# A seven-tile ring of weights for the second layer, and two read-backs issued a step later

## The chip, the cores and the metric

The kernel runs on one core of one Trainium2 chip. The metric is the device time of one execution in microseconds (us), as the median of the runs of a kernel. One further execution was taken with the hardware profiler; all rows shown here come from it.

## The reference

Causal attention in blocks of 64 over 4 batches of 8 heads (576 positions, head size 64) gives 2304 tokens of 512 numbers. Two gated layers follow, with 1536 hidden numbers each:

```python
x = attention(q, k, v)                      # 2304 x 512
x = (x @ w_a * (x @ w_b)) @ w_out           # first layer
xn = x / sqrt(mean(x * x) + 1e-6) * rms_g   # second layer
g = xn @ w_gate
y = (g * sigmoid(g) * (xn @ w_val)) @ w_out
```

All of it is fp32. The kernel reaches that accuracy by splitting each operand of a product into a high and a low part and adding three products: high by high, high by low, low by high.

## The kernel before

**Stages.** Tokens lie on the free axis. The first layer runs in five blocks of 512, 256, 512, 512 and 512 tokens, with the attention of the next batch beside each block but the last. The second layer runs in three blocks of 768 tokens. The table `blocks` holds all eight, and `before_fc` is called ahead of every tile of weights.

**Second layer.** `moe2` forms the two products of a pair of hidden groups by a scheme with seven half-size products instead of eight (`product`, lines L499 to L501 and L527 to L529). A half (`wi`) of a pair takes two tiles of weights: the even tile carries slots 0 to 3, the odd one slots 4 to 6. A slot is six matmuls of 384 columns, so an even tile feeds 24 matmuls and an odd one 18. The results are added on VectorE (L521 to L547, with ScalarE's copy L518 ahead of them), gated (L552 to L559) and split (L98, L108). Every three hidden groups `output` (L431 to L433, 72 matmuls) adds into `acc`; the results of a block leave by L744, `finish`.

**Weights.** `fetch_ab` loads a tile of the second layer from DRAM (`ab<-wc`, L227): 1024 KB for an even tile, 768 KB for an odd one. The pool `wab` has three tiles. `before_fc(fc)` fetches tile `fc + 2`, whose place is that of tile `fc - 1`. `fetch_o` (L231) loads 1536 KB of output weights at tiles 0, 4, 12 and 20 of a block.

**Norm.** While a block runs, the generator `normed` prepares the next block of the second layer, one step at each tile (two steps at each tile of the first layer). It loads the tokens (`xf`, L679), squares and sums them, puts the row of means in DRAM (`row<-sq`, L699), reads it back across partitions (`sm<-row`, L701), takes the root, puts the roots in DRAM (`row<-sm`, L709) and reads them back to all partitions (`y<-row`, L710). Then four multiplications `xf` (L714) and four sums (L636) follow on VectorE, and the split of seven operands. Each read-back stands right behind its write on the queue of SyncE (SP), which issues every transfer of this kernel in order.

**Order.** The tile framework simulates the program and writes out one order for each engine; an instruction waits there for its inputs and holds up what stands behind it. `behind(ins, "gate")` keeps an instruction behind the last gating instruction on VectorE in that order, without a semaphore.

**Memory.** `wab` and `stage` (tiles for decoding the weights, unused in the second layer) are opened for the whole kernel. The pools of the first layer are closed when the second begins, and `hp2`, `tp2` and `acc2` open on their place.

Of the kernel before, what the change touches and what calls it, by code (L numbers as in the profile page):

```python
# [9 lines left out]
F32R = mybir.dt.float32r  # L10
# [6 lines left out]
P = 128  # L17
# [28 lines left out]
def tile_attention_moe_moe(  # L46
# [13 lines left out]
    pe, act, dve, pool, sp = nc.tensor, nc.scalar, nc.vector, nc.gpsimd, nc.sync  # L60
# [5 lines left out]
    KC = DM // P  # L66
# [9 lines left out]
    const = ctx.enter_context(tc.tile_pool(name="const", bufs=1))  # L76
    wab = ctx.enter_context(tc.tile_pool(name="wab", bufs=3))
    wop = ctx.enter_context(tc.tile_pool(name="wop", bufs=2))
    stage = ctx.enter_context(tc.tile_pool(name="stage", bufs=2))
    dram = ctx.enter_context(tc.tile_pool(name="dram", bufs=1, space=bass.MemoryType.DRAM))  # L80
    x2_dram = dram.tile([P, KC, NT], F32, name="x2_dram")

# [114 lines left out]
        elif y == (1 if kind == "ab" else TF - 1):  # L197
            sp.dma_start(out=wab_dram[f] if kind == "ab" else wo_dram[layer][f], in_=t.bitcast(F32))

    quarters = {}  # L200

    def combine(pair, y, src):

# [14 lines left out]

    def fetch_ab(layer, n):

        t = wtiles["ab", n] = wab.tile([P, 4, KC * P], F32R, tag="ab", name="ab")
        if layer == 0:
            sp.dma_start(out=t.bitcast(F32), in_=wab_dram[n])
        else:
            pair, y, a = n // 4, n // 2 % 2, n % 2 * 4
            z = min(a + 4, NC)
            sp.dma_start(out=t[:, 0:z - a, :].bitcast(F32), in_=wc_dram[pair][y][:, a:z, :])  # L227
# [360 lines left out]
    BMAX = [max(n for l, _, n, _ in blocks if l == x) for x in range(2)]  # L588

    make_identity(nc, ident)  # L590
    first_layer = ctx.enter_context(ExitStack())
    hp = first_layer.enter_context(tc.tile_pool(name="hp", bufs=TF + 1))
    tp = first_layer.enter_context(tc.tile_pool(name="tp", bufs=2))
    xs = first_layer.enter_context(tc.tile_pool(name="xs", bufs=1))
# [80 lines left out]
    def normed(t0, n, parts):  # L675

        xr, ps_r = rms["sb"], rms["ps"]
        x = xr.tile([P, KC, BMAX[1]], F32, tag="xf", name="xf")[:, :, 0:n]
        sp.dma_start(out=x, in_=x2_dram[:, :, t0:t0 + n])  # L679
        sq = xr.tile([P, BMAX[1]], F32, tag="sq", name="sq")[:, 0:n]  # L680
        y = xr.tile([P, BMAX[1]], F32, tag="y", name="y")[:, 0:n]
        behind(act.activation(sq, x[:, 0, :], AF.Square), "hh")
        for c in range(1, KC):
            act.activation(y, x[:, c, :], AF.Square)
            dve.tensor_tensor(sq, sq, y, ALU.add)
            if c == 2:
                yield None
        sh = xr.tile([P, BMAX[1]], F32R, tag="sh", name="sh")[:, 0:n]
        sl = xr.tile([P, BMAX[1]], F32R, tag="sl", name="sl")[:, 0:n]
        split(sh, sl, sq, act, dve, "hh")  # L690
        yield None

        row, small = dram.tile([2, n], F32, name="row"), xr.tile([P, 3, n // P], F32, tag="sm", name="sm")
        for o, w in parts:
            ps = ps_r.tile([P, 512], F32, tag="r", name="r")
            pe.matmul(ps[:, 0:w], rms["ones"], sh[:, o:o + w], start=True, stop=False)
            pe.matmul(ps[:, 0:w], rms["ones"], sl[:, o:o + w], start=False, stop=True)
            dve.tensor_scalar(sq[0:1, o:o + w], ps[0:1, 0:w], 1.0 / DM, 1e-6, ALU.mult, ALU.add)
        sp.dma_start(out=row[0:1, :], in_=sq[0:1, :])  # L699
        v, r, t = (small[:, x, :] for x in range(3))  # L700
        sp.dma_start(out=v, in_=row[0, :].rearrange("(p n) -> p n", p=P))  # L701
        yield None
        behind(act.activation(r, v, AF.Sqrt), "hh")
        dve.reciprocal(r, r)
        dve.tensor_tensor(t, r, r, ALU.mult)
        dve.tensor_tensor(t, t, v, ALU.mult)
        dve.tensor_scalar(t, t, -0.5, 1.5, ALU.mult, ALU.add)
        dve.tensor_tensor(r, r, t, ALU.mult)
        sp.dma_start(out=row[1, :].rearrange("(p n) -> p n", p=P), in_=r)  # L709
        sp.dma_start(out=y, in_=row[1, :].partition_broadcast(P))  # L710
        yield None
        for c in range(KC):
            behind(
                dve.scalar_tensor_tensor(x[:, c, :], x[:, c, :], rms_g[:, c:c + 1], y, ALU.mult, ALU.mult),  # L714
                "gate",
            )
            yield None
        for b in sums_of(x):
            yield b
        if t0 == blocks[NB_FIRST][1]:  # L720

            res = {}
            for _ in split_sums(b, res):
                yield res
# [4 lines left out]
    for at, (layer, t0, n_tok, parts) in enumerate(blocks):  # L729
        following = blocks[at + 1] if at + 1 < len(blocks) else None  # L730
        with_attention = at + 1 < NB
        if layer == 1 and blocks[at - 1][0] == 0:
            first_layer.close()
            hp = ctx.enter_context(tc.tile_pool(name="hp2", bufs=6))
            tp = ctx.enter_context(tc.tile_pool(name="tp2", bufs=1))
            accs = ctx.enter_context(tc.tile_pool(name="acc2", bufs=1))
        acc = accs.tile([P, KC, BMAX[layer]], F32, tag="acc", name="acc")
        norm = normed(*following[1:]) if following and following[0] == 1 else iter(())
        got = {}

        def finish(dm, o, n, acc=acc, layer=layer, t0=t0):
            cols = slice(t0 + o, t0 + o + n)
            dst = x2_dram[:, dm, cols] if layer == 0 else out[dm * P:(dm + 1) * P, cols]
            sp.dma_start(out=dst, in_=acc[:, dm, o:o + n])  # L744

        n_tiles = (FC, 2 * FC)[layer]

        def before_fc(fc, n_tiles=n_tiles, at=at, layer=layer, following=following, norm=norm, got=got):
            if at == 0:
                if fc > 0:  # L750
                    for _ in range(TF):
                        if prepared[0] < len(w_pieces) // 2:
                            prepare()
            else:
                if layer == 1 and fc in (0, 4, 12, 20):
                    fetch_o(layer, (0, 4, 12, 20).index(fc))
                if layer == 0 and fc % TF == 0:
                    fetch_o(layer, fc // TF)
                if fc + 2 < n_tiles:
                    fetch_ab(layer, fc + 2)  # L760
                if layer == 0:
                    n = sum(BACKGROUND[:at]) + min(BACKGROUND[at], BACKGROUND[at] * (fc + 1) // (FC - 3))
                    while prepared[0] < len(w_pieces) // 2 + n:
                        prepare()
            if following and fc + 2 >= n_tiles:
                fetch_ab(following[0], fc + 2 - n_tiles)
            if fc >= 1:
                for _ in range(FC * 2 // n_tiles):
                    got["x"] = next(norm, None) or got.get("x")

        def before_last(at=at, layer=layer, following=following, got=got, norm=norm):
            if following is None:
                return iter(())
            if following[0] == 0:
                last = (following[1] + following[2] - 1) // S
                while done.get(last, 0) < H:
                    att.step()
            if following[0] == 0:
                got["split"] = split_of(*following[1:3])
            elif layer == 0:  # L780
                got["split"] = got["x"]
                assert len(got["x"]) == 7 and next(norm, 0) == 0
            else:
                got["split"] = {}
                assert "T4" in got["x"]
                return split_sums(got["x"], got["split"])
            return iter(())

        main = Stream((moe1, moe2)[layer]((hp, tp), nxt, parts, mm, acc, finish, before_fc, before_last))
        a0 = att.spent  # L790
        while main.step():
            while (
                with_attention
                and done.get(at + 1, 0) < H
                and att.spent - a0 < PACE[at] * main.spent
            ):
                with tc.high_priority(AHEAD[at]):
                    att.step()
        nxt = got.get("split")
        if at == NB - 2:  # L800
            while att.step():
                pass
            attn.close()
            xr = ctx.enter_context(tc.tile_pool(name="xr", bufs=1, side="right"))
            rms["sb"] = xr
            rms["ps"] = ctx.enter_context(tc.tile_pool(name="psr", bufs=2, space=PSUM, side="right"))
            mm_pools.append(ctx.enter_context(tc.tile_pool(name="psm2", bufs=3, space=PSUM, side="right")))
            ones = xr.tile([P, P], F32, name="ones")
            rms["ones"] = xr.tile([P, P], F32R, name="ones_r")
            pool.memset(ones, 1.0)  # L810
            dve.tensor_copy(rms["ones"], ones)
# [58 lines left out]
```

## Time and profile before

| | |
|---|---|
| median of 3 runs | 1141.39 us (1140.19 to 1143.38) |
| profiled execution, its own time | 1145.9 us |
| its span, first to last instruction | 1144.0 us |
| mean granted TensorE clock | 0.987 |
| TensorE matmuls busy | 1085.2 us, 95% |
| VectorE busy | 747.2 us, 65% |
| ScalarE busy | 525.3 us, 46% |
| GpSimd busy | 466.5 us, 41% |

Matmuls overlap and their ends are modelled, so the busy time of TensorE overstates how full it is. The second layer runs from about 702 us to the end.

### The profile page before, as it was taken

Reading aid. Unit: us, or ns where it says so; the run is one execution under the profiler, and the core shown is the slowest. Engines: PE = TensorE matmul, PEld = TensorE weight load, DVE = VectorE, ACT = ScalarE, POOL = GpSimd, SP = SyncE. Lnnn points to the kernel's source line nnn. Section 1 sums busy time; section 2 is a strip of 40 time slices with the busy share of each in tenths; the row PEclk is TensorE's granted clock in tenths of the full one; section 3 lists DMA queues with packets and bytes.
Section 4 is the critical chain, followed back from the end, with each engine's and each line's share of the span. In section 5 each row is a group of like instructions: output and inputs, shape, how many; then the busy total and the mean of one; then the engine's idle time right before and its main releaser. Section 6 shows DMA issues by size and latency. Waiting matters only on the chain.

```text
span 1144.0 us, 16235 instructions
## 1 busy us (share of the span) xinstructions
PE 1085.2 (95%) x5780; PEld 958.1 (84%) x5780; DVE 747.2 (65%) x1379; ACT 525.3 (46%) x1142; POOL 466.5 (41%) x460
## 2 busy tenths in 40 slices
PE   6889989999999999899999999999998899999998
PEld 4567767789888778688888778999998899999998
DVE  5888897856776767544646585755775755765564
ACT  5877876746556665325325434431423222223120
POOL 5766677534555665345434351221312212222120
PEclk9999999899999999999999999999999999999999
DMA  6544887868886867969979877845666457475551
GB/s 173 185 152 162 253 267 248 297 235 275 300 291 228 281 244 267 345 243 364 345 266 346 332 283 270 274 177 190 251 242 213 166 184 243 166 262 193 184 213 56
DMA packets 74280, 276.48 MB, mean 242 GB/s; under 512 B 25684, under 2 KB 33364, under 8 KB 56279
## 3 DMA queue, kind: packets, MB, share of 16 engines
q1 hardware_dynamic: 74198, 275.44, 68.4%
q8 instruction: 46, 0.75, 0.3%
q14 instruction: 36, 0.29, 0.1%
HBM read 218.77 MB, written 56.64 MB: 241 GB/s over the span
## 4 chain that ended last, share of the span: by engine, by line
PE 59%; DMA 15%; DVE 11%; POOL 6%; ACT 5%; issue 3%; SPq 0%; POOLq 0%; ACTq 0%; DVEq 0%
PE mm L433 7%; PE mm L431 7%; PE mm L432 7%; DMA ab<-wc 5%; PE mm L469 5%; PE mm L471 5%; PE mm L470 5%; PE mm L499 5%; DMA st<-in_w_ab_dram 5%; PE mm L500 5%; PE mm L501 5%; PE s L305 3%; POOL x L139 2%; DMA st<-in_w_o_dram 2%; DVE st L138 2%
## 5 line engine op out<-in xcount | busy, mean ns | idle before, releaser
L431 PE MATMUL mm<-hh,o 128*128 128x384 f32 (+2 forms) x528 | 190.5, 363 | 6.2 <-ACT hh L98 3.3
L432 PE MATMUL mm<-hh,o 128*128 128x384 f32 (+2 forms) x528 | 187.9, 357 | 0.0
L469 PE MATMUL mm<-xh,ab 128*128 128x512 f32 (+1 forms) x480 | 181.9, 382 | 3.0 <-DVE xh L100 1.0
L470 PE MATMUL mm<-xl,ab 128*128 128x512 f32 (+1 forms) x480 | 182.1, 380 | 0.0
L471 PE MATMUL mm<-xh,ab 128*128 128x512 f32 (+1 forms) x480 | 180.6, 377 | 0.0
L433 PE MATMUL mm<-hl,o 128*128 128x384 f32 (+2 forms) x528 | 179.5, 356 | 0.6 <-DVE hl L108 0.6
L108 POOL TENSOR_TENSOR hl<-g,hh 128x384 fp32r<-128x384 f32 (+2 forms) x76 | 89.6, 1179 | 174.2 <-ACT hh L98 157.1
L98 ACT ACTIVATE hh<-g 128x384 fp32r<-128x384 f32 (+2 forms) x132 | 71.1, 553 | 157.1 <-DVE g L559 95.7
L554 POOL TENSOR_TENSOR asb<-c,sig 128x384 f32<-128x384 f32 x36 | 36.8, 1022 | 224.4 <-ACT sig L552 204.1
L329 POOL TENSOR_SCALAR pp<-pp,st 128x64 f32<-128x64 f32 (+3 forms) x144 | 87.3, 621 | 78.5 <-DVE st L326 44.5
L431 PEld LDWEIGHTS mm<-hh,o 128*128 128x128 f32 x528 | 100.4, 190 | 18.6 <-ACT hh L98 5.0
L499 PE MATMUL mm<-hT,ab 128*128 128x384 f32 x288 | 99.4, 345 | 11.1 <-DMA ab<-wc 10.1
L469 PEld LDWEIGHTS mm<-xh,ab 128*128 128x128 f32 x480 | 91.4, 191 | 20.2 <-DVE acc L440 1.7
L305 PE MATMUL s<-ks,qz 128*128 128x384 f32 (+4 forms) x284 | 97.4, 433 | 11.4 <-ACT pp L314 11.2
L433 PEld LDWEIGHTS mm<-hl,o 128*128 128x128 f32 x528 | 99.8, 190 | 9.7 <-DVE hl L108 1.3
L432 PEld LDWEIGHTS mm<-hh,o 128*128 128x128 f32 x528 | 100.6, 190 | 8.8 <-issue 1.6
L471 PEld LDWEIGHTS mm<-xh,ab 128*128 128x128 f32 x480 | 91.1, 190 | 16.4 <-issue 0.7
L470 PEld LDWEIGHTS mm<-xl,ab 128*128 128x128 f32 x480 | 91.2, 190 | 16.2 <-issue 0.7
L440 DVE SCALAR_TENSOR_TENSOR acc<-mm,acc 128x384 f32<-128x384 f32 (+2 forms) x132 | 74.6, 588 | 42.4 <-PE mm L433 42.2
L501 PE MATMUL mm<-hT,ab 128*128 128x384 f32 x288 | 97.1, 337 | 0.0
L500 PE MATMUL mm<-lT,ab 128*128 128x384 f32 x288 | 96.9, 337 | 0.0
L314 ACT ACTIVATE pp<-s,st 128x288 f32<-128x288 f32 (+8 forms) x142 | 71.3, 505 | 40.5 <-DVE st L308 36.7
(128 smaller groups left out, 2343.5 us busy)
## 6 DMA issues: line engine op xcount, KB each, us to landing
ab<-wab SPq DMA_DIRECT2D x48, 1024.0 KB, 7.2
o<-wo SPq DMA_DIRECT2D x28, 1536.0 KB, 7.7
ab<-wc SPq DMA_DIRECT2D x36, 1024.0 KB, 6.9
ab<-wc SPq DMA_DIRECT2D x36, 768.0 KB, 4.4
st<-in_w_ab_dram SPq DMA_DIRECT2D x48, 512.0 KB, 4.6
wc<-bg SPq DMA_DIRECT2D x12, 1792.0 KB, 8.0
wab<-ab SPq DMA_DIRECT2D x12, 1024.0 KB, 4.9
st<-in_w_o_dram SPq DMA_DIRECT2D x24, 512.0 KB, 4.5
```

The source lines that it names most:

```text
L108: eng_lo.tensor_tensor(lo, src, hi.bitcast(F32), ALU.subtract)
L305: pe.matmul(ps[:, 0:z - a], qz[m % 2][:, b], ks[m][:, a:z], start=True, stop=True)
L329: pool.tensor_scalar(t, t, s[:, 10 + y:11 + y], 1.0, ALU.mult, ALU.mult)
L431: pe.matmul(ps[:, 0:n], wh, hh, start=(y == 0), stop=False)
L432: pe.matmul(ps[:, 0:n], wl, hh, start=False, stop=False)
L433: pe.matmul(ps[:, 0:n], wh, hl, start=False, stop=(y == TF - 1))
L469: pe.matmul(ps[:, 0:n], wh[:, a:z], xhc, start=(c == 0), stop=False)
L470: pe.matmul(ps[:, 0:n], wh[:, a:z], xlc, start=False, stop=False)
L471: pe.matmul(ps[:, 0:n], wl[:, a:z], xhc, start=False, stop=(c == KC - 1))
L499: pe.matmul(ps[:, 0:n], wh, xh[:, c, :], start=(c == 0), stop=False)
L500: pe.matmul(ps[:, 0:n], wh, xl[:, c, :], start=False, stop=False)
L501: pe.matmul(ps[:, 0:n], wl, xh[:, c, :], start=False, stop=(c == 1))
```

## The change

`stage` moves into the group of pools that is closed when the second layer begins. A pool `wab2` of four tiles opens on its place, and the tiles of the second layer go round seven places: three of `wab`, four of `wab2`. In the second layer `before_fc(fc)` fetches tile `fc + 6` instead of `fc + 2`; at the first tile of its first block it also fetches tiles 2 to 5, so that five fetches stand there. In `normed` each of the two read-backs is issued one step after its write, and stands behind the gating instruction of that step in the planned order. The norm so has two steps more, and all that follows the read-backs comes one or two steps later.

```diff
-    stage = ctx.enter_context(tc.tile_pool(name="stage", bufs=2))
+    first_layer = ctx.enter_context(ExitStack())
+    stage = first_layer.enter_context(tc.tile_pool(name="stage", bufs=2))
...
-    quarters = {}
+    quarters, rings, n_ring = {}, [], [0]
...
-        t = wtiles["ab", n] = wab.tile([P, 4, KC * P], F32R, tag="ab", name="ab")
+        ring = wab
+        if layer == 1:
+
+            n_ring[0] += 1
+            if n_ring[0] % 7 > 3 or n_ring[0] % 7 == 0:
+                ring = rings[0]
+        t = wtiles["ab", n] = ring.tile([P, 4, KC * P], F32R, tag="ab", name="ab")
...
-    first_layer = ctx.enter_context(ExitStack())
...
-        sp.dma_start(out=v, in_=row[0, :].rearrange("(p n) -> p n", p=P))
+        yield None
+        behind(sp.dma_start(out=v, in_=row[0, :].rearrange("(p n) -> p n", p=P)), "gate")
...
-        sp.dma_start(out=y, in_=row[1, :].partition_broadcast(P))
+        yield None
+        behind(sp.dma_start(out=y, in_=row[1, :].partition_broadcast(P)), "gate")
...
             first_layer.close()
+            rings.append(ctx.enter_context(tc.tile_pool(name="wab2", bufs=4)))
...
-                if fc + 2 < n_tiles:
-                    fetch_ab(layer, fc + 2)
+                if layer == 1 and rings and fc == 0 and blocks[at - 1][0] == 0:
+                    for i in range(2, 6):
+                        fetch_ab(layer, i)
+                ahead = 2 if layer == 0 else 6
+                if fc + ahead < n_tiles:
+                    fetch_ab(layer, fc + ahead)
...
-            if following and fc + 2 >= n_tiles:
-                fetch_ab(following[0], fc + 2 - n_tiles)
+            ahead = 2 if layer == 0 else 6
+            if following and fc + ahead >= n_tiles:
+                fetch_ab(following[0], fc + ahead - n_tiles)
```

## Rows read from the trace of the kernel before

**Rows 1.** Busy time by stage (three blocks of the second layer; one full stretch).

```profile
core 0: us, PE busy (x) PEld busy (x) DVE busy (x) ACT busy (x) POOL busy (x), PEclk, DMA share, GB/s
702.00:848.00 146.00, 143.48 (x814) 140.68 (x813) 98.32 (x171) 48.37 (x86) 30.43 (x26) 1.00 0.63 221
848.00:994.00 146.00, 135.91 (x756) 133.39 (x754) 93.40 (x164) 42.31 (x79) 30.55 (x26) 0.98 0.58 204
994.00:1143.00 149.00, 145.96 (x831) 143.41 (x830) 80.83 (x150) 33.63 (x68) 24.69 (x24) 1.00 0.50 182
760.00:780.00 20.00, 20.00 (x116) 19.81 (x116) 7.15 (x14) 5.01 (x10) 2.03 (x2) 1.00 0.49 171
```

**Rows 2.** Waits: who waited for whom, us in total, times, longest.

```profile
PE mm L499 <- DMA ab<-wc: 11.5, 9, 3.1
...
PEld mm L499 <- DMA ab<-wc: 13.1, 18, 3.5
```

**Rows 3.** Timeline of TensorE: start, duration, instruction, idle time before it and its releaser.

```profile
884.87 0.34 PE L501 MATMUL mm<-hT,ab 128*128 128x384 f32 x1
888.35 0.45 PE L499 MATMUL mm<-hT,ab 128*128 128x384 f32 x1 [3.15 <-DMA ab<-wc]
...
897.81 0.41 PE L499 MATMUL mm<-hT,ab 128*128 128x384 f32 x1 [2.43 <-DMA ab<-wc]
```

**Rows 4.** Busy time by stage, two stretches behind such waits; columns as in the first group.

```profile
862.00:865.00 3.00, 3.00 (x12) 3.00 (x11) 1.66 (x3) 0.00 (x0) 0.00 (x0) 0.51 0.04 7
889.00:892.00 3.00, 3.00 (x12) 3.00 (x12) 3.00 (x7) 0.82 (x2) 0.00 (x0) 0.56 0.08 33
```

**Rows 5.** Timeline of SP's queue at the second block's begin.

```profile
851.14 0.33 SPq L744 DMA_DIRECT2D out_dram<-acc  x1
853.45 1.54 SPq L227 DMA_DIRECT2D ab<-wc  x2
...
876.24 0.32 SPq L709 DMA_DIRECT2D row<-sm  x1
881.26 0.32 SPq L710 DMA_DIRECT2D y<-row  x1
881.67 22.97 SPq L227 DMA_DIRECT2D ab<-wc  x6
```

**Rows 6.** Issues from 690 us on: count, size, median us to landing.

```profile
ab<-wc SPq DMA_DIRECT2D x35, 1024.0 KB, 6.9
ab<-wc SPq DMA_DIRECT2D x36, 768.0 KB, 4.4
...
y<-row SPq DMA_DIRECT2D x2, 384.0 KB, 8.3
```

**Rows 7.** Timeline of VectorE, second block.

```profile
886.46 2.87 DVE L714 SCALAR_TENSOR_TENSOR xf<-xf,rms_g,y 128x768 f32<-128x768 f32 x3 [4.07 <-DMA y<-row]
...
896.99 0.55 DVE L543 TENSOR_TENSOR c<-p,mm 128x384 f32<-128x384 f32 x1
```

**Rows 8.** Timeline of SP's queue where the layers meet.

```profile
689.54 0.57 SPq L679 DMA_DIRECT2D xf<-x_dram  x1
691.30 5.76 SPq L227 DMA_DIRECT2D ab<-wc  x2
...
706.66 2.09 SPq L744 DMA_DIRECT2D x_dram<-acc  x3
711.03 1.88 SPq L227 DMA_DIRECT2D ab<-wc  x2
```

**Rows 9.** Timeline of ScalarE there.

```profile
698.30 0.85 ACT L684 ACTIVATE y<-xf 128x768 f32<-128x768 f32 x1 [3.62 <-DMA xf<-x_dram]
...
706.01 0.49 ACT L518 ACTIVATE p<-mm 128x384 f32<-128x384 f32 x1
```

**Rows 10.** Busy time by stage in the first layer's last block; columns as in the first group.

```profile
620.00:640.00 20.00, 19.78 (x87) 15.88 (x86) 9.94 (x22) 10.44 (x19) 8.64 (x8) 1.00 0.98 376
660.00:680.00 20.00, 17.84 (x71) 13.52 (x70) 18.98 (x19) 9.45 (x14) 13.22 (x8) 0.94 0.65 246
```

## The prediction

> **What bounds the kernel now.** I read the busy time by stage first. Where nothing disturbs TensorE, 116 matmuls take 20.00 us, that is 0.1724 us from start to start [rows 1]. The three blocks of the second layer show 814, 756 and 831 matmuls in 146, 146 and 149 us. At 0.1724 us they would need 140.3, 130.3 and 143.3 us. So TensorE loses 5.7, 15.7 and 5.7 us, 27 us in all, and only this can be won there: TensorE bounds the layer, and VectorE is busy for 98 of 146 us at most. The count of instructions on TensorE doesn't change.
>
> The list of waits says what the loss is made of. The first matmul of a tile (L499) idled nine times for the tile's transfer, 11.5 us together, and the weight load did so 18 times [rows 2]. The timeline shows how to size one wait: the last start before it is 884.87, the next 888.35, so 3.48 us instead of 0.17, a loss of 3.31 where the list shows 3.15; the first matmul then takes 0.45 instead of 0.34 us [rows 3]. So each of the nine costs about 0.27 us more than its idle time: 11.5 + 9 x 0.27 = 13.9 us. For the nine times in which only the weight load idled I take 0.25 us each, the same overhead: 2.2 us. Transfers that come late thus cost 16.1 us.
>
> Behind the two longest the clock fell. From 862 to 865 us and from 889 to 892 us only 12 matmuls fit into 3 us, at a granted clock of 0.51 and 0.56, which is the 1.2 GHz level [rows 4]; at 0.1724 us they need 2.07 us. That is 0.93 us in each. The low spacing reaches beyond these 3 us to some 11 matmuls with 0.15 us more each, so I take 1.6 us a place, 3.2 us together. Late tiles so cost 19.3 of the 27 us.
>
> Why they are late, SP's queue tells [rows 5]. A tile needs 4.4 to 6.9 us from issue to landing [rows 6], and with three places its fetch can't be issued before the tile three earlier is read, so it has the time of two tiles (42 matmuls, 7.2 us). Whatever holds SP up then goes straight to TensorE. At 853.45 two fetches leave behind the results of the block before (L744). At 876.24 the row of roots is written, and SP stands until 881.26 for it to land before it may issue the read-back; the fetch behind it leaves at 881.67, lands 6.7 us later, and that is the 3.31 us stall.
>
> **The change part by part.** *The ring.* Fetch and place keep their relation: tile fc + 6 is asked for when tile fc - 1 is read, at the same moment as before. What changes is that the tile is needed four tiles later, 4 x 21 x 0.1724 = 14.5 us. The longest stall is 3.31 us and the longest hold-up of SP shown is 5 us, so every late tile inside a block is covered three times over. At a block's border tiles 0 to 5 are there before the last 144 matmuls of output. Bytes and issues stay the same, and the 16 engines are busy for 0.50 to 0.63 of the blocks [rows 1]. Gain: up to 19.3 us.
>
> *What VectorE takes back.* At 897.81 the idle of 2.43 us is put down to a tile, but in the same moment VectorE ends L543 (896.99 + 0.55 = 897.54), which TensorE needs too, since it empties a bank of sums. VectorE is late because it stood 4.07 us for the row of roots (y) and then had four multiplications of 0.95 us and four sums to make [rows 7]. With the tile there, this stall stays unless the norm moves. I charge its 2.43 + 0.27 us, and 0.7 us for VectorE waits that the faster TensorE uncovers elsewhere: 3.4 us. The bounds are 0 (the two steps' delay puts the burst where `output` leaves VectorE idle: 7.15 of 20 us busy from 760 to 780 us, [rows 1]) and the whole loss there, 3.31 + 2.70 + 1.6 = 7.6 us.
>
> *The read-backs.* The same two small transfers and the same y of 384 KB; moved past the fetches of one step. What they free on SP is the 5 us above and its like; the ring hides the same hold-ups, so I count it at nothing beside the ring. Without the ring it would be worth the stall at 888.35, 3.31 + 1.6 us. The cost of the move is that y lands later, and the multiplications behind it are planned later too, by the same two steps (2 x 21 x 0.1724 = 7.2 us of a block with 23 steps, of which 15 are used): nothing. In the first layer's last block the 22 steps are all used now, and the split of the seven operands moves one tile back. There VectorE is busy 18.98 of 20 us from 660 to 680 us, and TensorE loses 2.2 us of busy time and clock (0.94) worth 1.2 us [rows 10]. This may shrink or grow by its own size, 3.4 us either way; I take 0.
>
> *The place of* `stage`. It has no user in the second layer. Its last users are background transfers in the first layer's last block; I take 0, and bound a wait for them by one landing, 6.9 us [rows 6], hidden by tiles 0 to 2, which last 3 x 21 x 0.1724 = 10.9 us.
>
> Sum: 19.3 - 3.4 = 15.9 us less. The profiled execution took 1145.9 us, so 1130.0 us for one like it. The median of the runs is 0.9961 of that execution: 1141.39 - 15.9 = **1125.5 us**.
>
> **The rivals.** *VectorE keeps more.* All of the 7.6 us stay, and the uncovered waits double: 19.3 - 7.6 - 1.4 = 10.3 us less, 1131.1 us. For it: TensorE, freed of tiles, comes to VectorE's burst sooner. Against it: the burst moves towards `output`.
>
> *The burst where the layers meet.* Tiles 3 to 6 (3.67 MB) are asked for at once. At 376 GB/s, the fastest 20 us shown [rows 10], they take 9.8 us. Today `xf` goes out at 689.54 ahead of two fetches [rows 8], and ScalarE waits 3.62 us for it until 698.30, with L518 of the first product behind it in order at 706.01 [rows 9]. If the four tiles go first, ScalarE stands up to 9.8 us longer; TensorE can fill six banks of six matmuls, 6.2 us, before it must wait. Price 3.6 to 9.8 us with the clock; I take 7: 1132.5 us. Against it: the tiles stand after the block's begin in the program and after the two that today leave from 691.30 on. On this the Trainium skill (DMA: Bandwidth & Descriptors, Queues, rings and completion order) says that each DMA engine consumes a queue's descriptors in ring order, so a small transfer would wait for all that was issued ahead. The trace leans to it: y of 384 KB took 8.3 us to land, longer than a tile of 1024 KB [rows 6].
>
> *The change doesn't do it.* SP stays held behind results and writes, and tiles come as late as before, or the gain is given back at the border: within 3.4 us of 1141.4. Against it: no hold-up of 14.5 us stands ahead of a fetch in rows 5.
>
> *Slower.* VectorE's first multiplication keeps its place in the planned order while y comes two steps later, 7.2 us. Its wait of 4.07 us becomes 11.3 us, TensorE runs out of banks after 6.2 us and then falls to the low clock. That happens at three places (one norm in the first layer, two in the second). At 7.2 + 1.6 us each it costs 26 us and eats the gain: 1125.5 + 26.4 = 1151.9 us. It decides from 19.3 / 3 = 6.4 us a place on. Against it: the multiplications come behind y in the program by as many steps as before.
>
> **How the numbers follow.** Forecast 0.60, VectorE keeps more 0.14, burst 0.11, no change 0.06, slower 0.09. A measurement of this kernel can tell about 0.3% (3.4 us) from no change. Faster is 0.60 + 0.14 + 0.11 = 0.85, same 0.06, slower 0.09. The range begins at 19.3 us of late tiles plus 3.4 us of the first layer's last block, about 23 us, or 1118, less 1 for the tail; it ends above both rivals of the same sign at 1136. That leaves out no change, slower and a small tail below, under 0.2.
>
> **What would show it.** Right: no wait of L499 for `ab` above 0.5 us after 720 us, a clock of 1.00 in all three blocks, the second layer some 16 us shorter, the middle block by the most. SP would show other transfers between the write and the read of the row. Wrong, by rival: L543 or L521 in the place of the tile as releaser near the multiplications; ScalarE's first squares of the second layer waiting for `xf` past 700 us with TensorE idle behind L518; L714 waiting more than 6 us for y. Also wrong is a first layer that ends at another time than 702 us by more than 3.4 us.

## The result and the profile after

The changed kernel takes 1129.35 us (median of 5 runs, 1126.49 to 1130.21), the kernel before 1140.19 us beside it (5 runs). The ratio is 0.9893 with an interval of 0.9868 to 0.9917, so 12.2 us or 1.07% are won (the two medians lie 10.8 us apart), where 15.9 us were forecast. Executions of one program spread over some 11 us (17 runs of the kernel before: 1133.1 to 1144.6), and part of that arises ahead of the first layer's last block, where neither the ring nor the norm is at work. So I measure two stages besides the times: the *last block* of the first layer, from its first L470 matmul to the first matmul of the second layer, and the *second layer*, from there to the end of the last matmul. In the profile of before they take 102.2 us (599.8 to 702.0) and 438.7 us (702.0 to 1140.7), in that of after 98.4 us (594.9 to 693.3) and 428.0 us (693.3 to 1121.3). The three blocks of the second layer, each from its first matmul to the next one's, took 145.2, 153.4 and 140.1 us before and 147.5, 143.0 and 137.5 us after: the first got longer. Line numbers after are higher: L499 is L506 now, L521 is L528, L714 is L722, L227 is L234.

Busy time by stage of the kernel after, the three blocks, a stretch of the first layer's last block, and the stretch of the longest stall; columns as in [rows 1]:

```profile
core 0: us, PE busy (x) PEld busy (x) DVE busy (x) ACT busy (x) POOL busy (x), PEclk, DMA share, GB/s
694.00:836.00 142.00, 137.37 (x779) 136.29 (x778) 96.83 (x167) 46.31 (x84) 30.98 (x26) 0.99 0.63 234
836.00:978.00 142.00, 139.17 (x792) 138.53 (x791) 97.58 (x169) 45.25 (x83) 29.75 (x26) 0.99 0.63 227
978.00:1121.00 143.00, 143.00 (x827) 143.00 (x825) 79.30 (x148) 33.30 (x68) 24.46 (x24) 1.00 0.44 158
...
660.00:680.00 20.00, 19.90 (x88) 16.03 (x87) 13.30 (x18) 8.90 (x14) 11.40 (x8) 1.00 0.77 294
...
740.00:760.00 20.00, 16.18 (x84) 15.86 (x83) 14.06 (x20) 5.64 (x13) 3.13 (x3) 0.91 0.35 141
```

The last block of the second layer runs without a gap now: 827 matmuls in 143 us are 0.1729 us each. The first two still lose, and the clock falls to 0.91 in the stretch of the longest stall. The waits of TensorE say to whom (all of the second layer, as in [rows 2]):

```profile
PE mm L438 <- DVE u L528: 3.8, 1, 3.8
PE mm L506 <- DVE u L528: 1.9, 1, 1.9
PE mm L506 <- DVE u L545: 0.9, 1, 0.9
PE mm L506 <- DMA ab<-wc: 0.8, 1, 0.8
```

Of 11.5 us for tiles 0.8 are left; VectorE took their place. TensorE's timeline at the longest one, which answers to [rows 3], and VectorE's in both norms, which answers to [rows 7]:

```profile
741.35 0.34 PE L536 MATMUL mm<-hB,ab 128*128 128x384 f32 x1
745.50 0.44 PE L438 MATMUL mm<-hh,o 128*128 128x384 f32 x1 [3.82 <-DVE u L528]
```

```profile
741.00 3.98 DVE L722 SCALAR_TENSOR_TENSOR xf<-xf,rms_g,y 128x768 f32<-128x768 f32 x4 [2.99 <-DMA y<-row]
744.91 0.54 DVE L528 TENSOR_TENSOR u<-p,mm 128x384 f32<-128x384 f32 x1
...
873.49 1.02 DVE L722 SCALAR_TENSOR_TENSOR xf<-xf,rms_g,y 128x768 f32<-128x768 f32 x1 [1.25 <-DMA y<-row]
...
875.83 3.64 DVE L722 SCALAR_TENSOR_TENSOR xf<-xf,rms_g,y 128x768 f32<-128x768 f32 x3
879.39 0.54 DVE L528 TENSOR_TENSOR u<-p,mm 128x384 f32<-128x384 f32 x1
```

VectorE stands 2.99 us for the row of roots, makes the four multiplications without a break, and only then L528, which empties the bank that TensorE needs. SP's queue answers to [rows 8] (first four lines) and to [rows 5] (last three):

```profile
679.25 6.64 SPq L234 DMA_DIRECT2D ab<-wc  x6
686.26 0.57 SPq L685 DMA_DIRECT2D xf<-x_dram  x1
688.06 0.33 SPq L234 DMA_DIRECT2D ab<-wc  x1
695.51 0.92 SPq L753 DMA_DIRECT2D x_dram<-acc  x2
...
864.54 0.32 SPq L716 DMA_DIRECT2D row<-sm  x1
869.82 0.32 SPq L718 DMA_DIRECT2D y<-row  x1
870.20 8.26 SPq L234 DMA_DIRECT2D ab<-wc  x4
```

Two things are to be seen. In the second block the read-back still stands right behind its write: no fetch leaves between 864.54 and 869.82, though its step comes later. (In the first block fetches leave between write and read-back. They did so in the kernel before already, against what I wrote of it: at 728.00, between 727.58 and 729.03.) And seven fetches stand around `xf` where the layers meet.

### The profile page after: what moved, and what is told of

Read it like the earlier page. It is cut to its first block, busy times and chain, and to the rows that moved or that the text cites. A ratio compares the mean times of both kernels' runs of the same rounds, so it can differ in the third digit from the quotient of the medians.

```text
span 1124.7 us, 16248 instructions
## 1 busy us (share of the span) xinstructions
PE 1076.7 (96%) x5780; PEld 956.7 (85%) x5780; DVE 748.1 (67%) x1379; ACT 523.6 (47%) x1142; POOL 466.9 (42%) x460
## 4 chain that ended last, share of the span: by engine, by line
PE 66%; DMA 11%; DVE 10%; POOL 5%; ACT 4%; issue 3%; SPq 0%; POOLq 0%; ACTq 0%; DVEq 0%
PE mm L438 7%; PE mm L439 7%; PE mm L440 7%; PE mm L506 6%; PE mm L508 6%; PE mm L507 6%; PE mm L476 6%; PE mm L478 6%; PE mm L477 6%; PE s L312 3%; DMA st<-in_w_ab_dram 3%; DMA st<-in_w_o_dram 2%; DMA ab<-wc 2%; PE t L373 2%; PE t L347 2%
## 5 line engine op out<-in xcount | busy, mean ns | idle before, releaser
L438 PE MATMUL mm<-hh,o 128*128 128x384 f32 (+2 forms) x528 | 189.7, 363 | 8.0 <-DVE u L528 3.8
L109 POOL TENSOR_TENSOR hl<-g,hh 128x384 fp32r<-128x384 f32 (+2 forms) x76 | 87.1, 1146 | 157.9 <-ACT hh L99 156.9
L438 PEld LDWEIGHTS mm<-hh,o 128*128 128x128 f32 x528 | 100.4, 190 | 19.9 <-DVE u L528 4.1
L506 PE MATMUL mm<-hT,ab 128*128 128x384 f32 x288 | 97.1, 338 | 2.8 <-DVE u L528 1.9
L508 PE MATMUL mm<-hT,ab 128*128 128x384 f32 x288 | 95.0, 337 | 0.0
```

What stands on the lines that cost most here:

```text
L109: eng_lo.tensor_tensor(lo, src, hi.bitcast(F32), ALU.subtract)
L438: pe.matmul(ps[:, 0:n], wh, hh, start=(y == 0), stop=False)
L506: pe.matmul(ps[:, 0:n], wh, xh[:, c, :], start=(c == 0), stop=False)
L508: pe.matmul(ps[:, 0:n], wl, xh[:, c, :], start=False, stop=(c == 1))
```

## The experiments

**The ring alone.** Both read-backs go back to their old place; the ring of seven stays.

```diff
-        yield None
-        behind(sp.dma_start(out=v, in_=row[0, :].rearrange("(p n) -> p n", p=P)), "gate")
+        sp.dma_start(out=v, in_=row[0, :].rearrange("(p n) -> p n", p=P))
...
-        yield None
-        behind(sp.dma_start(out=y, in_=row[1, :].partition_broadcast(P)), "gate")
+        sp.dma_start(out=y, in_=row[1, :].partition_broadcast(P))
```

> The ring of seven without the move of the read-backs. Theory 'ring': late tiles are all that was won in the second layer, so the ratio to the kernel before is that of the full change, 0.986 to 0.992, and TensorE loses some 11 to 12 us in the second layer, at VectorE's multiplications, as with the full change. Rival 'read-backs': holding SP up for the row still costs; then this run is 5 us (0.4%) or more slower than the full change, and waits for tiles of more than 1 us come back behind the read-backs.

1131.55 us, ratio 0.994 (0.9917 to 0.9963). The second layer takes 427.5 us against 428.0, with the same stalls: 3.8 us at the first row of multiplications, 1.9 and 0.5 us at the second, 0.4 us for a tile. So in the second layer the ring does all. But the ratio is 0.0047 above that of the full change, some 5 us, though the two intervals touch. 2.3 us of them are seen: the last block of the first layer takes 100.7 us instead of 98.4. So the theory held for the second layer and missed its ratio; of the rival's two signs the slower time came, the waits for tiles above 1 us did not.

**The read-backs alone.** The kernel before with the two steps and the two `behind`, the read of `v` likewise.

```diff
-        sp.dma_start(out=y, in_=row[1, :].partition_broadcast(P))
+        yield None
+        behind(sp.dma_start(out=y, in_=row[1, :].partition_broadcast(P)), "gate")
```

> The read-backs a step later, three places for the tiles as before. Theory 'ring': ratio 0.997 to 1.003, the waits for tiles stay at 10 us or more together. Rival 'read-backs': the stall of 3.3 us behind the read-back of the second block and the low clock behind it go, some 5 us less, ratio near 0.995.

1141.67 us, ratio 1.0032 (1.0014 to 1.0050), just above the range of the first theory. The rival's gain did not come. Its waits in the second layer:

```profile
PE mm L499 <- DMA ab<-wc: 10.2, 8, 3.0
PE mm L499 <- DVE asb L554: 2.4, 2, 1.8
```

The stall behind the second block's read-back is still there (3.0 us at 885.68). The layer takes 438.9 us and the first layer's last block 98.5 us.

**Four places.** One tile in the second pool, fetched three ahead.

```diff
-            if n_ring[0] % 7 > 3 or n_ring[0] % 7 == 0:
+            if n_ring[0] % 4 == 0:
...
-                    for i in range(2, 6):
+                    for i in range(2, 3):
...
-                ahead = 2 if layer == 0 else 6
+                ahead = 2 if layer == 0 else 3
```

> The full change with four places instead of seven (one tile in the second pool, fetched three ahead). A tile then has one tile's time more than before, 3.6 us, and the longest wait before was 3.3 us. Theory 'one more is enough': ratio within 0.003 of the full change's 0.989, no wait for a tile above 1 us. Rival 'depth': hold-ups of SP of 5 us and the border need more; half of the 12 us comes back, ratio 0.994 or more.

1127.19 us, ratio 0.9895 (0.9872 to 0.9918); second layer 428.4 us.

```profile
PE mm L506 <- DVE u L545: 6.0, 2, 3.7
PE mm L506 <- DMA ab<-wc: 0.6, 1, 0.6
```

One place more does what four do. The other three were worth nothing that can be measured here.

**The multiplications spread.** A gate is set twice in each half of a pair, and the multiplications start four steps later, each behind the gate of its own step. The sums stand behind the same gate.

```diff
-                dve.tensor_tensor(u1, p1, p6, ALU.add)
+                gate["step"] = dve.tensor_tensor(u1, p1, p6, ALU.add)
...
-                dve.tensor_tensor(u3, u1, p7, ALU.add)
+                gate["step"] = dve.tensor_tensor(u3, u1, p7, ALU.add)
...
         behind(sp.dma_start(out=y, in_=row[1, :].partition_broadcast(P)), "gate")
+        for _ in range(0 if t0 == blocks[NB_FIRST][1] else 4):
+            yield None
...
-                "gate",
+                "step" if "step" in gate else "gate",
```

> The full change, and in the second layer's norms the four multiplications by the row of roots are planned four steps later and one to a step instead of one behind another. Theory 'burst': what TensorE still loses in the second layer (11 us of 12) is VectorE standing for the row and then making 4 us of multiplications in one go; with them apart at least 6 of these 11 us go, ratio 0.981 to 0.985. Rival 'sum of work': VectorE is short of time around the norm whatever the order, the stalls move and stay within 3 us of their sum, ratio 0.987 to 0.992.

1119.02 us, ratio 0.9824 (0.9800 to 0.9847). The second layer takes 418.4 us, 9.6 us less than with the full change; no wait for VectorE is left, and one for a tile (1.6 us where the layers meet). VectorE's timeline in the first norm:

```profile
742.53 0.55 DVE L528 TENSOR_TENSOR u<-p,mm 128x384 f32<-128x384 f32 x1 [0.97 <-ACT p L525]
744.17 1.58 DVE L724 SCALAR_TENSOR_TENSOR xf<-xf,rms_g,y 128x768 f32<-128x768 f32 x1 [1.08 <-DMA y<-row]
...
746.60 1.01 DVE L724 SCALAR_TENSOR_TENSOR xf<-xf,rms_g,y 128x768 f32<-128x768 f32 x1
```

L528, which TensorE needs, now comes ahead of the first multiplication, and the other three stand between the sums (746.60, 760.60, 762.61). VectorE is busy for as long as with the full change (273.0 us of the second layer against 273.7), so it was its order, not its sum. How much of it is the four steps and how much the one to a step was not run apart.

**The kernel before, again, and the changed one.**

> The kernel before, unchanged, for a second profile. If its second layer is the same each time, its first matmul to its last end takes 438.7 us again to within 1 us, with the waits for tiles at the same places, and only the part ahead of it moves between executions. If the late tiles are chance, the sum of their waits (11.5 us) changes by several us.

> The kernel before, a third profile. The first two gave 438.7 and 433.4 us for the second layer, with waits for tiles that differ behind the second block's read-back (3.3 and 1.0 us). Theory 'late by chance': the third lies between 432 and 440 us, with other sizes at the same places. If the first was an exception, 432 to 434 us.

> The changed kernel, a second profile. Its first gave 428.0 us for the second layer, with stalls behind VectorE only. These hang on the planned order and little on when transfers land, so 428 us to within 2 us, with stalls of 3 to 5 us at both rows of multiplications, and 98 to 99 us for the first layer's last block.

The kernel before gave 433.4 and 432.2 us for the second layer (438.7 at first) and 100.1 and 101.6 us for the last block (102.2); the changed one 428.3 us (428.0) and 98.9 us (98.4). The waits for tiles, second profile and third:

```profile
PE mm L499 <- DMA ab<-wc: 7.7, 10, 2.4
```

```profile
PE mm L499 <- DMA ab<-wc: 7.1, 7, 2.3
```

The stall behind the read-back, 3.31 us in [rows 3], was 0.98 and 1.53 us here. Late tiles are partly chance, and the profile that the prediction read had the most of three. Whether it was an exception, three profiles don't tell: 432.2 us fits both theories of the third. VectorE's stalls are not: 3.82, 2.19 and 0.95 us in the second profile of the changed kernel.

**Without the wait for the row.** In the changed kernel the multiplications read the row of sums.

```diff
-                dve.scalar_tensor_tensor(x[:, c, :], x[:, c, :], rms_g[:, c:c + 1], y, ALU.mult, ALU.mult),
+                dve.scalar_tensor_tensor(x[:, c, :], x[:, c, :], rms_g[:, c:c + 1], y if t0 == blocks[NB_FIRST][1] else sq, ALU.mult, ALU.mult),
```

> The full change, but in the second layer's norms the four multiplications read the row of sums, which lies ready in SBUF, in the place of the row of roots; the row of roots is still read back. So VectorE never stands for the row, and the norm of two blocks is numerically another. Theory 'wait': VectorE's 3 us wait for the row is what TensorE pays for; its stalls at the multiplications fall from 4 and 3.2 us to under 1 us each. Theory 'burst': the four multiplications in one go keep a stall of 1 to 3 us wherever they are planned.

```profile
PE mm L506 <- DVE u L528: 3.7, 2, 2.1
PE mm L506 <- DVE u L545: 1.0, 2, 0.6
PE mm L506 <- DMA ab<-wc: 0.9, 1, 0.9
```

1123.51 us in one run; second layer 423.4 us, 4.6 less than with the full change. Stalls of 1.6 and 2.1 us remain at the two rows of multiplications, and the low clock is gone. So 'burst' came true and 'wait' did not; but the wait is worth 4.6 us, about half of what VectorE costs. The planned order moved with the edit, too: the first stall stands at L506 now, not at L438.

**Without the multiplications.** The four are left out in the same two norms.

```diff
         for c in range(KC):
-            behind(
+            if t0 == blocks[NB_FIRST][1]:
+              behind(
```

> The full change without the four multiplications in the second layer's norms of its last two blocks, which so work on tokens that aren't scaled. Both theories of VectorE (its wait for the row, its multiplications in one go) expect that no stall of TensorE above 1 us is left around the norm, and a second layer of 417 to 420 us in the place of 428. If VectorE's sums and squares matter as much, stalls of 2 us or more stay.

1114.19 us in one run; second layer 418.3 us, and no stall but 1.6 us for a tile. That is the 418.4 us of the spread multiplications: planned apart, they cost TensorE nothing that can be seen here.

**The places handed out in another order.** The spread kernel still waits once for a tile. With seven places as in the change, tile 2 gets the third old place, which the first layer's last tile frees. Its fetch leaves last, at 688.06 in the rows above, and lands 16.1 us later; the profile after shows TensorE's wait for it:

```profile
704.35 0.42 PE L506 MATMUL mm<-hB,ab 128*128 128x384 f32 x1 [0.82 <-DMA ab<-wc]
```

Now tiles 2 to 5 get the new pool and tile 6 that place.

```diff
-            if n_ring[0] % 7 > 3 or n_ring[0] % 7 == 0:
+            if n_ring[0] % 7 > 2:
```

> The kernel with the multiplications spread, and the places handed out in another order: tiles 2 to 5 of the layer's begin get the new pool, tile 6 the third old place, so that tile 2 needn't wait for the first layer's last tile to be read. Theory 'order of places': the one stall left there, 1.7 us for tile 2, goes, the second layer takes 416 to 417 us in the place of 418.4, ratio 0.979 to 0.983. Rival 'burst at the border': tile 1, which now leaves last of the six, is late instead, with a stall of 1 us or more at the layer's begin.

1116.99 us, ratio 0.9799 (0.9773 to 0.9825), the fastest of the kernels that leave nothing out. The second layer takes 416.4 us, and the list of TensorE's waits is empty there. Busy time by stage of this kernel:

```profile
695.00:834.00 139.00, 139.00 (x798) 138.40 (x797) 96.65 (x168) 47.60 (x86) 31.01 (x26) 1.00 0.67 249
834.00:973.00 139.00, 139.00 (x803) 139.00 (x803) 97.86 (x171) 43.37 (x81) 29.96 (x26) 1.00 0.63 228
973.00:1112.00 139.00, 138.82 (x801) 138.50 (x799) 77.98 (x146) 33.30 (x68) 24.41 (x24) 1.00 0.45 160
```

798, 803 and 801 matmuls in 139 us are 0.173 to 0.174 us each: TensorE alone bounds the layer. Tile 1, now the last of the six that leave ahead of `xf`, was in time; the one that leaves behind `xf`, at 690.19, is by the order of the places tile 6, which isn't needed before 720.76.

**The first layer's norm as before.** The same kernel, but without the two steps in the norm that the first layer's last block makes; the read of `y` likewise. The two `behind` go in all three norms.

```diff
-        yield None
-        behind(sp.dma_start(out=v, in_=row[0, :].rearrange("(p n) -> p n", p=P)), "gate")
+        if t0 != blocks[NB_FIRST][1]:
+            yield None
+        sp.dma_start(out=v, in_=row[0, :].rearrange("(p n) -> p n", p=P))
```

> The best kernel so far, but in the first layer's last block both read-backs are issued right behind their writes again, so the norm made there has its two steps fewer; in the second layer the steps stay. Theory 'steps': what the move of the read-backs won is that the norm's later work in that block comes one tile later; the block takes 100 to 101 us again in the place of 98.2, ratio 0.981 to 0.984. Rival 'chance': the block's length only varies between executions; 98 to 99 us and a ratio within 0.001 of 0.980.

1118.64 us, ratio 0.9818 (0.9793 to 0.9843): its interval overlaps that of the best kernel, so the times alone don't tell. The stage does: 101.1 us against 98.2. The other four profiles with the old norm there (three of the kernel before, one of the ring alone) give 100.1 to 102.2 us, all nine profiles with the two steps 98.1 to 99.0. Busy time from 660 to 680 us, to be held against [rows 10] and the 19.90 us above:

```profile
660.00:680.00 20.00, 17.88 (x76) 13.63 (x75) 17.86 (x18) 9.12 (x15) 13.25 (x8) 1.00 0.64 242
```

**Spread without the ring.** Three places, read-backs moved, multiplications spread with the same edit.

> The kernel before with the read-backs moved and the multiplications spread, but with three places for the tiles. Theory 'two causes': late tiles and VectorE's burst each stall TensorE by themselves; the waits for tiles stay at 8 us or more, those for VectorE near the multiplications go, the second layer takes 432 to 437 us, ratio 0.993 to 1.000. Rival 'VectorE alone': with VectorE in time the tiles are in time too, and the second layer comes below 425 us.

1136.33 us, ratio 0.9986 (0.9962 to 1.0010); second layer 433.9 us, where the kernel before takes 432.2 to 438.7.

```profile
PE mm L499 <- DMA ab<-wc: 9.7, 7, 2.4
```

No wait for VectorE is on its list, but the tiles are as late as ever. The ring and the spread multiplications each remove one cause, and only with both does TensorE run through.

## Why the prediction came out as it did

The direction was right, both mechanisms of the sum were at work, and the time lies in the range; that it came so near is partly luck. The forecast was 3.9 us too low. Its sum was 19.3 - 3.4 + 0; each of the three terms was off in size: the first two promised too much, the third too little. All of the 15.9 us were to be won in the second layer. On the means of the profiles (three of before, two of the change) that layer got 6.6 us shorter, less than half; 2.7 us came from the first layer's last block, which the sum put at nothing, and 2.6 us lie ahead of both, where the three profiles of the kernel before differ by 3.6 us among themselves.

**Late tiles, 19.3 us.** This rested on one execution, the worst of three. Added from start to start, the stalls above 0.2 us at tiles were 13.7, 10.7 and 8.6 us in the three profiles of before, and 1.0 and 1.2 us with the change. So the ring removed nearly all of what there was, but on the mean of three (11.0 us) that was some 3 us less than in the profile that was read. Even there the sum had charged 16.1 us for these waits: it counted the longer first matmul (0.11 us each), which is no loss from start to start, and nine more waits where only 12 stalls in all are above 0.2 us. Nor did the clock fall behind the two longest: it fell behind the waits of 3.15 and 2.29 us, not behind that of 2.43 us at 897.81. What the ring is worth by itself the third block shows, which has no norm beside it: 140.0 to 140.4 us in the three profiles of before, 137.5 us in all eight with seven places. The best kernel, which waits for nothing there, shows the floor: 416.4 us. Against it the three profiles lose 22.3, 17.0 and 15.8 us, not the 27 that I read from the counts (2.3 of the 27 lie behind the last matmul, which ends at 1140.7), and the changed kernel 11.6. The remaining 1 us is tile 2 at the border, where I had written that tiles 0 to 5 would be there; that holds for the borders between blocks of the second layer, not for its begin.

**What VectorE takes back, 3.4 us.** This is the step that failed most. VectorE's stall at the first norm cost 3.98 us from start to start, the two at the second 2.05 and 1.11 us, and the low clock and the refilled pipeline behind them 3.4 us: some 10.5 us. Spreading gave back 9.6 us. My upper bound for the stretch was 7.6 us, since I looked at the second block alone; in the first, no stall of that kind was above 0.90 us before, yet its stall became the longest. The argument that the later steps move the burst towards `output`, where VectorE is idle, did not help: the multiplications ended up right ahead of `output` in the first block, whose first matmul (L438) then waited for 3.82 us. The ring alone has the same wait of 3.8 us there, so the later steps neither made it nor helped. A step only says from when on an instruction may be planned, and in the planned order of the first block the four stand side by side. That they do because their steps had all passed when the planner let the row land is argued, not shown; that their order is the cause of the stalls, the spread kernel shows.

**The read-backs, 0 us.** In the second layer 0 was right, but not for my reason. I took them to be moved past the fetches of one step; in the second block the read-back still follows its write, and SP stood from 864.54 to 869.82 as it had from 876.24 to 881.26 in [rows 5]. The ring made that harmless. In the first layer's last block I took 0 with bounds of 3.4 us; it was a gain of 2 to 3 us (100.1 to 102.2 us against 98.1 to 99.0), the stretch of [rows 10] became one of 19.90 us busy at a clock of 1.00, and *norm as before* ties it to the move of the read-backs in that norm, steps and `behind` together. In all five profiles with the old norm TensorE is busy there for 17.84 to 17.98 us; the low clock, which I charged with 1.2 us, stands in two of the five (0.94 and 0.91).

**The rivals.** *VectorE keeps more* named the right mechanism and a loss of 5.6 us against my forecast; 12.2 us won lies between that rival (10.3) and the forecast (15.9). *The burst* came about and cost 1 us, not 7, and by another way. `xf` went out at 686.26 behind six fetches and landed for ScalarE's first square only at 701.06, 14.8 us later against 8.8 before [rows 8, 9]. This agrees with the Trainium skill (DMA: Bandwidth & Descriptors, Queues, rings and completion order): each engine takes descriptors in the order of the ring. But ScalarE's row shows why TensorE didn't feel this wait:

```profile
697.33 0.49 ACT L525 ACTIVATE p<-mm 128x384 f32<-128x384 f32 x1 [7.80 <-PE mm L508]
701.06 0.85 ACT L688 ACTIVATE sq<-xf 128x768 f32<-128x768 f32 x1 [3.25 <-DMA xf<-x_dram]
```

The copy that empties the first product (L525) was planned ahead of the squares this time. What the burst cost is the wait for tile 2, the last of it: 0.98 us. It also made the norm of the first block later: `xf` came 7.7 us behind the layer's begin instead of 3.7 us ahead of it, and the row of roots was read back 42.1 us behind the begin (735.45) instead of 27.0 (729.03). Whether this is what put the four multiplications right ahead of `output`, no run separates. *Slower* did not come: the longest wait for the row was 3.18 us in the first layer's last block (3.12 there before) and 2.99 us in the second layer, not 11.3. *The change doesn't do it* is excluded for the second layer by the ring alone.

**The signs.** No wait for a tile above 0.5 us after 720 us and the middle block shortened by the most: these came. A clock of 1.00 in all blocks, 16 us in the second layer and other transfers between the write and the read-back of the second block did not come, and L528 (L521 before) as the releaser is the sign of *VectorE keeps more*. The first layer ended 8.7 us earlier, which I had called a sign of being wrong; 4.9 us of that lie ahead of its last block.

What stays open: the read-backs alone were slower by 0.3% although the first layer's last block got shorter. Its second layer took 438.9 us, at the upper end of the three of before; with one profile of it I can't say whether the later norm makes tiles later.

## What to carry to other kernels

Before a deeper ring, ask what the engine needs next when the tile is there: here a second cause stood behind the first, and it grew when the first went. One place more was enough: it gives the time of one tile (21 x 0.1724 = 3.6 us), and the longest wait was 3.15 us [rows 3]. With the ring in place the planned order of four multiplications was then worth more (9.6 us of the second layer) than the whole change had been (6.6 us there, on the means); without the ring it could not be told from nothing. Take the size of waits for transfers from more than one execution, and compare stages when the part ahead of them varies more than the effect.

## What was not expected of the hardware

The clock fell to its 1.2 GHz level behind a single wait of 2.29 us (0.51 from 862 to 865 us, [rows 4]) and again behind VectorE's stalls of 1.89 and 0.94 us close together (0.91 over 880 to 900 us), but not in the run without the wait for the row, whose stalls of 2.11 and 0.48 us lay as close. The second and third profile of the kernel before have a wait of the same size at the same place, 2.28 and 2.34 us, and the clock stayed at 1.00 behind it; there it fell behind the waits of 2.38 and 2.26 us some 32 us later. So a stall of 2 us can cost nearly as much again (1.6 us by the count in the prediction), and doesn't always; its size alone doesn't tell.

The part of the program ahead of the first layer's last block ended between 591.3 and 599.8 us over fourteen profiles, while the block ahead of that one took 99.5 to 99.6 us in each of them. What varies there so lies in the first 500 us, where the attention runs: the block ahead of the last has none beside it either, against what I wrote of the stages. The rest of the spread is in the stages themselves: over the three profiles of the kernel before, the second layer varied by 6.5 us and the last block by 2.1.
